# A transformer block's prologue: x's third tile on another queue, its statistics earlier, its copies split by features

## The chip, the cores and the metric

The kernel runs on one core of a Trainium2 chip. The metric is the device time of one execution in microseconds; smaller is better. The engines are named as in the profile: PE is TensorE (PEld its weight loads), DVE VectorE, ACT ScalarE, POOL GpSimd, SP SyncE. SyncE and ScalarE issue the transfers (DMAs), each on a queue of its own.

## The reference

x has 2048 rows of 576 bf16 elements. The block normalises x once and adds three terms:

```python
xn = _layernorm(x)                       # (x - mean) / sqrt(var + 1e-5), by rows
qkv = (xn @ wqkv)                        # 576 -> 3 * 576, 32 heads of 18
p = softmax(where(0 <= i - j < 256, q @ k.T * 18**-0.5, -1e9))
A = (p @ v) @ wo
B = (silu(xn @ w1) * (xn @ w3)) @ w2     # 576 -> 4608 -> 576
out = x + A + B
```

## The kernel before

**Tiling.** The 2048 rows are worked through in four chunks of 512, and a chunk in four tiles of 128 rows. For each chunk: V, q and k are projected (L491), then 36 units of the feed-forward's first half run (L759), with the attention's scores (L621), exponentials and products with V (L689) dealt between them, then the second half and the output (L832). The normalised rows are needed transposed, features on the partitions: `xnT`. From the second chunk on, this preparation happens under the work of the chunk before. For the first chunk nothing lies before it, and a prologue written out by hand does it. The change lies there.

**Order.** Every operation is put by `add` into one list; each engine runs its own operations in the order of that list, and waits on semaphores that are worked out from which buffers an operation reads and writes. So each engine is a queue in which one waiting instruction holds up all behind it.

**The prologue**, tiles 0 to 3 of x:

- `load_x` (L304) asks for a tile of 128 rows: tile 0 on SyncE's queue, tiles 1, 2, 3 on ScalarE's. SyncE's queue goes on with V's weights `wv` (L890, L894), then those of q and k (L920, L924; in the trace their target is `pt`), and later the feed-forward's (L328). GpSimd copies each tile's last 64 columns (L963), in tile order, as soon as it lands.
- `ln_stats` (L394, L397): VectorE takes the statistics of a tile in two halves of 288 columns and joins them. Tile 1's are taken by ScalarE instead (L385, L388). `ln_sqrt` (L367): ScalarE takes the root. `normalise`: VectorE takes its reciprocal (L372) and scales the tile (L411). The small buffers (`stats`, `mv`, `rstd`, `sd`) are two each, by turns.
- `xn_turn` (L426, L439): TensorE transposes a tile in ten small matmuls (five blocks of 128 features, each for two halves of 64 rows) into PSUM, and two copies bring it to `xnT`. A copy takes either some of the features of all 128 rows (blocks 0 and 1, or 2 to 4, each from a bank pair of its own), or, with `by_rows`, all features of 64 rows, both from one pair. Before the change tiles 0 and 1 are copied by features, both copies on ScalarE; tiles 2 and 3 by rows, one copy on ScalarE, one on VectorE.
- `proj_begin` and `proj_end`: V of a tile is 18 matmuls (L491), eight in a first part, ten in a second; the second part is put behind the transposes of the next tile. The first part takes feature blocks in order, two matmuls each, and waits for blocks 0 and 1 by one key (`xnTa`), for 2 and 3 by another (`xnTb`). V of a tile needs a bank pair until VectorE and ScalarE have moved it to `va` in four steps (L540, L542); those steps are kept in the lists `moves` and `late` and put where the code says.
- PSUM has eight banks, used in pairs: `JOBS[0]`, `JOBS[1]`, `JOBS[2]`, and `SC` (banks 6 and 7). `job()` hands the three pairs of `JOBS` out in turn.
- Ahead of all this, matmuls on constants (L902, L908, L914) fill TensorE's time. Behind V come q and k (L491 too, from `wp`), for which GpSimd deals the weights out (L946). `xn_swap` (L454) makes `xnS`, `xnT` with its partition halves exchanged, for the feed-forward.

The order around the change, before (the first `ln_stats` line of tile 2 and the `xn_turn` of tiles 2 and 3 are what moves or changes):

Of the kernel before, what the change touches and what calls it, by code (L numbers as in the profile page):

```python
# [5 lines left out]
dt = mybir.dt  # L6
# [38 lines left out]
class _Prog:  # L45
# [13 lines left out]
    def add(self, eng, fn, r=(), w=(), j=(), dma=None, after=()):  # L59
        deps = []  # L60
        for k in r:
            deps += self.bufs[k].writers
        for k in w:
            g = self.bufs.get(k)
            if g is not None:
                deps += g.ahead(eng)
        for k in j:
            g = self.bufs[k].before
            if g is not None:
                deps += g.ahead(eng)  # L70
        op = _Op(eng, fn, deps + list(after), dma)
        op.after = tuple(after)
        self.n[eng] += 1
        op.pos = self.n[eng]
        if dma is not None:
            self.dma_count[dma] = self.dma_count.get(dma, 0) + 16
            op.cnt = self.dma_count[dma]
        for k in r:
            self.bufs[k].readers.append(op)
        for k in w:  # L80
            self.bufs[k] = _Gen([op], self.bufs.get(k))
        for k in j:
            self.bufs[k].writers.append(op)
        for k in w:
            if self.bufs[k].before is not None:
                self.bufs[k].before.before = None
        self.ops.append(op)
        return op
# [76 lines left out]
def bass_parallel_sum__sliding_block__glu_gated_swiglu__prompt_kernel(  # L165
# [23 lines left out]
    HD = D // 2  # L189
# [6 lines left out]
    add = P.add  # L196

    with ExitStack() as es:

        def sb(name, shape, dtype=dt.bfloat16):  # L200
            return es.enter_context(nc.sbuf_tensor(name, shape, dtype))
# [4 lines left out]
        ident = sb("ident", [128, 128])  # L206
        xp = [sb(f"xp{i}", [128, 640 if i < TB else D]) for i in range(NXP)]
        xn = [sb(f"xn{i}", [128, 640]) for i in range(2)]
        stats = [sb(f"stats{i}", [128, 2, 6], dt.float32) for i in range(2)]
        mv = [sb(f"mv{i}", [128, 2], dt.float32) for i in range(2)]  # L210
        vpe = [sb(f"vpe{i}", [128, 1], dt.float32) for i in range(2)]
        rstd = [sb(f"rstd{i}", [128, 1], dt.float32) for i in range(2)]
# [66 lines left out]
        JOBS, SC = ((0, 1), (2, 3), (4, 5)), (6, 7)  # L279
# [3 lines left out]
        def job():  # L283
            ring.append(ring.pop(0))
            return ring[2]

        def half_bank(b):
            return PS[:, b, :].bitcast(dt.bfloat16)
# [11 lines left out]
        def load_x(t, eng="sp"):  # L300
            nonlocal xp_ctr
            s = xp_ctr % NXP
            xp_ctr += 1
            add(eng, lambda e: e.dma_start(xp[s][:, 0:D], x2[t * 128:(t + 1) * 128, :]), w=[("xp", s)], dma=f"xp{s}")  # L304
            return s
# [59 lines left out]
        def ln_sqrt(t, scale=1.0):  # L365
            i = t % 2
            add("act", lambda e: e.activation(sd[i][:], mv[i][:, 1:2], ACT.Sqrt, bias=eps[:], scale=scale),  # L367
                r=[("mv", i), "eps"], w=[("sd", i)])

        def ln_recip(t):  # L370
            i = t % 2
            add("dve", lambda e: e.reciprocal(rstd[i][:], sd[i][:]), r=[("sd", i)], w=[("rstd", i)])  # L372

        def ln_root(t):
            i = t % 2
            add("pool", lambda e: e.tensor_scalar(vpe[i][:], mv[i][:, 1:2], 1e-5, None, op0=ALU.add),
                r=[("mv", i)], w=[("vpe", i)])
            add("pool", lambda e: e.tensor_tensor(rstd[i][:], vpe[i][:], neghalf[:], ALU.pow),
                       r=[("vpe", i), "neghalf"], w=[("rstd", i)])
# [9 lines left out]
                r=[("xp", s), ("vpe", i)], w=[("mv", i), *keys])  # L389

        def ln_stats(t, s, part):
            i = t % 2
            if part < 2:
                add("dve", lambda e: e.bn_stats(stats[i][:, part, :], xp[s][:, part * HD:part * HD + HD]),  # L394
                    r=[("xp", s)], **{"j" if part else "w": [("stats", i)]})
                return
            op = add("dve", lambda e: e.bn_aggr(mv[i][:], stats[i][:]), r=[("stats", i)], w=[("mv", i)])  # L397
            if t >= TB:
                ln_root(t)
            return op  # L400
# [14 lines left out]
        def xn_turn(t, pairs, eng, between=(), by_rows=False):  # L415
            i = t % 2
            c, tt = divmod(t, TB)
            ranges = ((0, 2), (2, 5))
            for n, (k0, k1) in enumerate(ranges):
                for k in range(k0, k1):  # L420
                    for r in range(2):
                        r0 = 64 * r
                        b = pairs[n][r]
                        bv = half_bank(b)[:, 64 * k:64 * k + 64]
                        new = k == k0 and (n == 0 or pairs[0] != pairs[1])
                        add("pe", lambda e, bv=bv, r0=r0, k=k: e.transpose(  # L426
                            bv, xn[i][r0:r0 + 64, k * 128:(k + 1) * 128], ident[r0:r0 + 64, r0:r0 + 64],
                            tile_position=(r0, 0)),
                            r=[("xn" if k < 4 else "xnd", i), "ident"], **{"w" if new else "j": [("ps", b)]})
            for what in between:  # L430
                what()
            dst = xnT[:, c % 2, :, tt * 128:(tt + 1) * 128].rearrange("p k (r f) -> p k r f", f=64)
            for n, (k0, k1) in enumerate(ranges):
                b = pairs[n][0]
                src = PS[:, b:b + 2, :].bitcast(dt.bfloat16)[:, :, 0:320].rearrange("p r (k f) -> p k r f", f=64)
                d, s = dst[:, k0:k1, :, :], src[:, k0:k1, :, :]
                if by_rows:
                    d, s = dst[:, :, n, :], src[:, :, n, :]
                move = (lambda e, d=d, s=s: e.tensor_copy(d, s)) if eng[n] == "dve" else (lambda e, d=d, s=s: e.activation(d, s, ACT.Copy))  # L439
                add(eng[n], move, r=[("ps", b) for b in pairs[n]],  # L440
                    **({"j": [("xnT", c % 2, tt), ("xnTb", tt)] + [("xnTa", tt)] * by_rows} if n else
                       {"w": [("xnT", c % 2, tt), ("xnTa", tt), ("xnTb", tt)]}))
# [77 lines left out]
        def proj_end(later=None, late=None):  # L520
            if pend:
                c, what, banks, last = pend.pop()
                proj_part(c, what, banks, 1, last)
                proj_out(c, what, banks, later, late)
                return what

        def proj_begin(c, what, banks=None):
            banks = banks or job()
            last = proj_part(c, what, banks, 0)
            got = proj_end()  # L530
            pend.append((c, what, banks, last))
            return got
# [352 lines left out]

        xslot = {}
        for t in range(TB):
            xslot[t] = load_x(t, "act" if t else "sp")
        add("act", lambda e: e.preload_act_table_set("sqrt_and_others"))
        add("sp", lambda e: e.dma_start(  # L890
            wv[:, 0:4, :], A_wqkv[0:512, 2 * D:3 * D].rearrange("(kd p) f -> p kd f", p=128)),
            w=["wv"], dma="wv")
# [12 lines left out]
        def warm_halves(banks, cols):  # L905
            for r in range(2):
                rows = slice(64 * r, 64 * r + 64)
                add("pe", lambda e, b=banks[r], rows=rows, r=r: e.matmul(  # L908
                    PS[:, b, 0:cols], oq[rows, 0:128], oq[rows, 0:cols], start=True, stop=True, tile_position=(64 * r, 0)),
                    r=["oq0"], w=[("ps", banks[r])])  # L910
# [54 lines left out]
        moves, late = [], []  # L965
        for p in range(2):
            ln_stats(0, xslot[0], p)
# [4 lines left out]
        def normalise(t):  # L972
            ln_recip(t)
            ln_apply(t, xslot[t], (2,))

        normalise(0)
        xn_turn(0, (SC, JOBS[1]), ("act", "act"))
        for cols in (256, 256, 128):
            warm_halves(JOBS[0], cols)
        ln_stats(2, xslot[2], 0)  # L980
        ln_stats(2, xslot[2], 1)
        normalise(1)
        ln_stats(2, xslot[2], 2)
# [8 lines left out]
        proj_end(moves, late)  # L992
        proj_begin(0, ("v", 1))
        ln_sqrt(3)
        xn_turn(2, (SC, SC), ("act", "dve"), by_rows=True)
        normalise(3)
        moves.pop(0)()
        first = [late.pop(0)]
        proj_end(moves, late)
        proj_begin(0, ("v", 2))  # L1000
        xn_turn(3, (SC, SC), ("act", "dve"), first, by_rows=True)
        for move in moves + late:
            move()
        xn_swap(0, ("sp", "sp"))
        proj_end()
        proj_begin(0, ("v", 3), SC)
        deal_main(0, 0, 0, 2)
        deal_spread(0)
        deal_main(0, 1, 0, G)
# [47 lines left out]
        for c in range(NC):  # L1057
# [133 lines left out]
            for u in range(NF):  # L1191
# [11 lines left out]
                for n in range(9):  # L1203
# [9 lines left out]
                    op = unit_pairs(c, u, n, n + 1, b0[0])  # L1213
# [11 lines left out]
                if u in stat:  # L1225
                    t = (c + 1) * TB + stat[u]
# [4 lines left out]
                if u in apply:  # L1231
                    t = (c + 1) * TB + apply[u]
# [11 lines left out]
                if c == 0 and u == 18:  # L1244
                    rows = A_wo[0:4 * Dh, :].rearrange("(n d) f -> n d f", d=Dh)
                    add("sp", lambda e: e.dma_start(wo[126:128, 0:4, :], rows[:, 0:2, :].rearrange("n d f -> d n f")),
                        j=["wo"], dma="wo")
                    for p in range(2):
                        add("sp", lambda e, p=p: e.dma_start(wo[64 * p:64 * p + 64, 4, :], rows[:, 2:Dh, :]),
                            j=["wo"], dma="wo")  # L1250
# [13 lines left out]
            for item in p2_list(c):  # L1264
# [14 lines left out]
                elif n in (100, 120) and c + 2 < NC:  # L1279
                    t = (c + 2) * TB + (n == 120)  # L1280
# [34 lines left out]
```

## Time and profile before

| | us |
|---|---|
| three runs | 554.45, 554.74, 555.17 |
| their median | 554.74 |
| the profiled execution | 554.48 |
| its span in the trace | 552.7 |

| engine | busy us | share of the span |
|---|---|---|
| PE | 548.7 | 99% |
| PEld | 338.7 | 61% |
| DVE | 313.7 | 57% |
| ACT | 258.8 | 47% |
| POOL | 212.3 | 38% |

In the timeline's rows stand the start in microseconds from the span's start, the time from the first to the last of a group, the engine, the line, the operation, the tiles written and read, the shape and the count; in brackets, how long the engine was idle before it and what released it. The chain of waits lists, in order of time, the work that the end of the execution hung on. Rows of groups end in busy microseconds, mean nanoseconds of one instruction, and idle time before it. TensorE's clock was granted in full over the whole span.

### The profile page before, as it was taken

How to read it: one execution, taken by the hardware profiler on the slowest of the kernel's cores; microseconds unless marked ns; L12 is line 12 of the kernel's file. 1: busy time of each engine (PE TensorE's matmuls, PEld its weight loads, DVE VectorE, ACT ScalarE, POOL GpSimd, SP SyncE). 2: the span in 40 equal slices, each digit the busy share in tenths (PEclk: the TensorE clock that was granted, in tenths of full speed). 3: DMA queues.
4: the chain of work that ended last, by engine and by line, in shares of the span. 5: the costliest groups of instructions: out<-in, count | busy, mean ns of one | idle time of the engine just before them, and what ended most of it. 6: DMA issues, size and time to landing. Idle time of an engine off the chain costs nothing.

```text
span 552.7 us, 18355 instructions
## 1 busy us (share of the span) xinstructions
PE 548.7 (99%) x8071; PEld 338.7 (61%) x8071; DVE 313.7 (57%) x584; ACT 258.8 (47%) x360; POOL 212.3 (38%) x388
## 2 busy tenths in 40 slices
PE   8999999999999999999999999999999999999998
PEld 5555544777555544577765554559886555445776
DVE  8466797710468886651056988665105567866311
ACT  6456776000288567700047857760005784775000
POOL 6324675400047465530005656643001553663100
PEclk9999999999999999999999999999999999999999
DMA  9997899676577953758646875466763673541750
GB/s 253 209 199 167 197 221 202 138 200 182 141 144 145 177 135 102 176 143 208 182 111 140 172 146 146 112 155 167 194 179 87 138 173 102 152 110 52 195 152 23
DMA packets 128038, 86.00 MB, mean 156 GB/s; under 512 B 35702, under 2 KB 125646, under 8 KB 127958
## 3 DMA queue, kind: packets, MB, share of 16 engines
q1 hardware_dynamic: 89138, 62.80, 49.7%
q10 hardware_dynamic: 38820, 22.02, 15.7%
q8 instruction: 63, 1.03, 0.8%
q14 instruction: 17, 0.14, 0.1%
HBM read 71.29 MB, written 2.36 MB: 133 GB/s over the span
## 4 chain that ended last, share of the span: by engine, by line
PE 98%; DMA 1%; ACT 0%; DVE 0%; issue 0%
PE ps L759 51%; PE ps L832 29%; PE ps L491 10%; PE ps L621 6%; PE ps L689 3%; DMA xp<-in_A_x_dram 1%; DVE stats L394 0%; ACT hT L388 0%; ACT sd L367 0%; PE ps L426 0%; ACT xnT L439 0%; DVE ofin L854 0%; DVE mv L397 0%
## 5 line engine op out<-in xcount | busy, mean ns | idle before, releaser
L759 PE MATMUL ps<-xnT,w 64*128 64x512 bf16 x1400 | 185.3, 376 | 0.0
L759 PE MATMUL ps<-xnS,w 64*128 64x512 bf16 x1120 | 150.6, 376 | 0.0
L832 PE MATMUL ps<-w,hT 64*128 64x288 bf16 x2292 | 144.0, 282 | 0.0
L774 DVE SCALAR_TENSOR_TENSOR gs<-th,ps 128x512 bf16<-128x512 bf16 x144 | 97.9, 680 | 77.7 <-ACT th L768 77.2
L832 PEld LDWEIGHTS ps<-w,hT 64*128 64x128 bf16 x2292 | 117.1, 94 | 24.8 <-issue 0.2
L768 ACT ACTIVATE th<-ps 128x512 bf16<-128x512 f32 x144 | 85.7, 595 | 60.5 <-PE ps L759 59.3
L759 PEld LDWEIGHTS ps<-xnT,w 64*128 64x128 bf16 x1400 | 66.8, 94 | 63.7
L777 DVE SCALAR_TENSOR_TENSOR hT<-gs,ps 128x512 bf16<-128x512 bf16 x144 | 98.9, 687 | 5.0
L658 POOL TENSOR_TENSOR pt<-pt,mk 128x256 bf16<-128x256 bf16 (+1 forms) x143 | 85.6, 622 | 26.3 <-ACT pt L630 26.3
L630 ACT ACTIVATE pt<-ps 128x1024 bf16<-128x1024 f32 (+1 forms) x80 | 80.7, 1009 | 24.0 <-PE ps L621 23.3
L658 POOL TENSOR_TENSOR hT<-hT,mk 128x256 bf16<-128x256 bf16 (+1 forms) x52 | 30.3, 604 | 160.4 <-ACT hT L630 160.4
L759 PEld LDWEIGHTS ps<-xnS,w 64*128 64x128 bf16 x1120 | 53.6, 94 | 51.0
L504 ACT ACTIVATE stage<-ps 128x512 bf16<-128x512 f32 x16 | 9.6, 597 | 139.2 <-PE ps L491 139.2
L863 DVE TENSOR_TENSOR ofin<-ps,xp 128x288 bf16<-128x288 f32 x31 | 12.2, 451 | 98.2 <-PE ps L832 98.2
L621 PE MATMUL ps<-qv,kv 64*128 64x320 bf16 (+4 forms) x528 | 51.4, 260 | 0.0
L621 PEld LDWEIGHTS ps<-qv,kv 64*128 64x128 bf16 x528 | 26.2, 94 | 27.7 <-ACT pt L630 0.8
L491 PE MATMUL ps<-xnT,wp 64*128 64x512 bf16 (+1 forms) x360 | 38.4, 355 | 0.0
L722 DVE STREAM_TRANSPOSE od<-oq 128x256 bf16<-128x256 bf16 x64 | 25.4, 426 | 12.1 <-POOL oq L715 12.1
L630 ACT ACTIVATE hT<-ps 128x1024 bf16<-128x1024 f32 (+1 forms) x28 | 28.4, 1014 | 7.8 <-PE ps L621 7.6
L658 POOL TENSOR_TENSOR stage<-stage,mk 128x256 bf16<-128x256 bf16 (+1 forms) x44 | 24.9, 587 | 14.4 <-ACT stage L630 14.4
L630 ACT ACTIVATE stage<-ps 128x1024 bf16<-128x1024 f32 (+1 forms) x24 | 24.3, 1014 | 7.9 <-PE ps L621 7.8
L491 PEld LDWEIGHTS ps<-xnT,wp 64*128 64x128 bf16 x360 | 18.4, 94 | 14.3
(92 smaller groups left out, 394.2 us busy)
## 6 DMA issues: line engine op xcount, KB each, us to landing
w<-in_B_w_dram SPq DMA_DIRECT2D x210, 192.0 KB, 4.0
w<-in_B_w_dram ACTq DMA_DIRECT2D x70, 288.0 KB, 3.6
xp<-in_A_x_dram SPq DMA_DIRECT2D x29, 144.0 KB, 4.1
out_dram<-ofin SPq DMA_DIRECT2D x31, 72.0 KB, 2.0
xnS<-xnT SPq DMA_DIRECT2D x8, 256.0 KB, 5.0
oT<-od SPq DMA_DIRECT2D x56, 36.0 KB
pt<-in_A_wqkv_dram SPq DMA_DIRECT2D x4, 288.0 KB, 5.3
hT<-in_B_w_dram SPq DMA_DIRECT2D x6, 192.0 KB, 7.1
```

The lines of the kernel that those rows point to most:

```text
L491: op = add("pe", lambda e, out_=out_, st=st, mv=mv, n=n, r0=r0, first=first: e.matmul(out_, st, mv, start=first, stop=(part == 1 and n == ...
L621: add("pe", lambda e, r0=r0, out_=out_, kb=kb, q0=q0, nb=nb: e.matmul(out_, kb4[r0:r0 + 64, g, kb + NV - NB, :] if kb < 0 else kv[r0:r0 + ...
L630: add("act", lambda e: e.activation(pt_slot(sl)[:, :, 0:w], PS[:, SC[0]:SC[1] + 1, 0:w], ACT.Exp, scale=scale), r=[("ps", b) for b in SC], ...
L658: add("pool", lambda e, vb=vb, mm=mm: e.tensor_tensor(vb, vb, mm, ALU.mult), r=(key if n == 0 else []) + ["mk"], **{"w" if n == 0 else "j" ...
L689: add("pe", lambda e, p=p, q=q, pr=pr, sl=sl, g=g, pos=pos, q0=q0, nb=nb, col=col, first=first, n=n: e.matmul(PS[32 * q:32 * q + VW, banks ...
L722: add("dve", lambda e: e.transpose(od[i][:, g % 2, c0:c0 + CH // 2], oq[:, c0:c0 + CH // 2]), r=["oq", "oq0"], **{"j" if half or g % 2 els ...
L759: op = add("pe", lambda e, n=n, r0=r0, r=r, k=k, src=src: e.matmul(PS[:, b0 + r, :], wt[r0:r0 + 64, k, fl * 128:(fl + 1) * 128], src, star ...
L768: add("act", lambda e: e.activation(th[i][:], PS[:, bg, :], ACT.Tanh, scale=0.5), r=[("ps", bg)], w=[("th", i)])
L774: add("dve", lambda e: e.scalar_tensor_tensor(out=gs[i][:], in0=th[i][:], scalar=1.0, in1=PS[:, bg, :], op0=ALU.add, op1=ALU.mult), r=[("t ...
L777: add("dve", lambda e: e.scalar_tensor_tensor(out=hT[:, u, :], in0=gs[i][:], scalar=0.5, in1=PS[:, bu, :], op0=ALU.mult, op1=ALU.mult), r= ...
L832: op = add("pe", lambda e: e.matmul(PS[:, bank, 0:w], stat, move, start=new, stop=False, skip_group_check=True, **tile), r=keys, after=hel ...
L863: add("dve", lambda e: e.tensor_tensor(ofin[:, o, :], PS[:, bank, 0:HD], xp[xs[n]][:, d0:d0 + HD], ALU.add), r=[("ps", bank), ("xp", xs[n] ...
```

## The change

Four things are done in the prologue.

1. Tile 2 of x is asked for by SyncE, behind tile 0 and ahead of V's weights. ScalarE asks for tiles 1 and 3.
2. The first half of tile 2's statistics stands on VectorE ahead of tile 0's reciprocal, instead of behind tile 0's scaling. The statistics buffer has three copies for that.
3. Tile 2 is copied to `xnT` by features: blocks 0 and 1 by VectorE from `SC`, blocks 2 to 4 by ScalarE from `JOBS[1]`. Tile 3, still by rows, is transposed into `JOBS[1]`.
4. V of tile 2 is accumulated in `SC` and V of tile 3 in a pair of `JOBS` (it was the other way round), and two of the evacuations of V's tile 0 on ScalarE, not one, stand ahead of the copies of tile 3.

```diff
-        stats = [sb(f"stats{i}", [128, 2, 6], dt.float32) for i in range(2)]
+        stats = [sb(f"stats{i}", [128, 2, 6], dt.float32) for i in range(3)]
...
         def ln_stats(t, s, part):
-            i = t % 2
+            i, b = t % 2, t % 3
             if part < 2:
-                add("dve", lambda e: e.bn_stats(stats[i][:, part, :], xp[s][:, part * HD:part * HD + HD]),
-                    r=[("xp", s)], **{"j" if part else "w": [("stats", i)]})
+                add("dve", lambda e: e.bn_stats(stats[b][:, part, :], xp[s][:, part * HD:part * HD + HD]),
+                    r=[("xp", s)], **{"j" if part else "w": [("stats", b)]})
                 return
-            op = add("dve", lambda e: e.bn_aggr(mv[i][:], stats[i][:]), r=[("stats", i)], w=[("mv", i)])
+            op = add("dve", lambda e: e.bn_aggr(mv[i][:], stats[b][:]), r=[("stats", b)], w=[("mv", i)])
...
-            xslot[t] = load_x(t, "act" if t else "sp")
+            xslot[t] = load_x(t, "act" if t % 2 else "sp")
...
+        ln_stats(2, xslot[2], 0)
         normalise(0)
         xn_turn(0, (SC, JOBS[1]), ("act", "act"))
         for cols in (256, 256, 128):
             warm_halves(JOBS[0], cols)
-        ln_stats(2, xslot[2], 0)
         ln_stats(2, xslot[2], 1)
         normalise(1)
...
         ln_sqrt(3)
-        xn_turn(2, (SC, SC), ("act", "dve"), by_rows=True)
+        xn_turn(2, (SC, JOBS[1]), ("dve", "act"))
         normalise(3)
         moves.pop(0)()
-        first = [late.pop(0)]
+        first = [late.pop(0) for _ in range(2)]
         proj_end(moves, late)
-        proj_begin(0, ("v", 2))
-        xn_turn(3, (SC, SC), ("act", "dve"), first, by_rows=True)
+        proj_begin(0, ("v", 2), SC)
+        xn_turn(3, (JOBS[1], JOBS[1]), ("act", "dve"), first, by_rows=True)
         for move in moves + late:
             move()
         xn_swap(0, ("sp", "sp"))
         proj_end()
-        proj_begin(0, ("v", 3), SC)
+        proj_begin(0, ("v", 3))
```

## The prediction

> **What bounds the kernel now.** I read the page's head and chain first, then the chain of waits inside the first 22 us, because the diff touches nothing later.
>
> ```profile
> span 552.7 us, 18355 instructions
> PE 98%; DMA 1%; ACT 0%; DVE 0%; issue 0%
> ...
> 0.79 2.78 DMA xp<-in_A_x_dram
> 3.59 0.83 DVE stats L394 x2
> 4.45 0.22 DVE mv L397
> ...
> 5.78 0.30 ACT sd L367
> ...
> 6.52 0.71 PE ps L491 x8
> ...
> 10.20 10.59 PE ps L491 x118
> ```
>
> The first two lines are the page's: TensorE carries 98% of the chain. The rest (start, us, what) is the prologue. One tile of x has to land (3.57) and pass through statistics, root, normalising, transposing and a copy before V's first matmul at 6.52; from then on the chain lies on TensorE. So only two things can move the end: the start at 6.52, or holes in TensorE's queue behind it. The holes show where the same work takes unequal time:
>
> ```profile
> 7.30 1.28 PE L491 MATMUL ps<-wv,xnT 64*128 64x288 bf16 x18
> 8.41 0.31 PE L426 MATMUL ps<-ident,xn 64*128 64x64 bf16 x10
> 8.64 1.41 PE L491 MATMUL ps<-wv,xnT 64*128 64x288 bf16 x18
> 10.12 1.28 PE L491 MATMUL ps<-wv,xnT 64*128 64x288 bf16 x18
> 9.38 0.36 PEld L491 LDWEIGHTS ps<-wv,xnT 64*128 64x128 bf16 x8 [0.26 <-ACT xnT L439]
> ```
>
> These are TensorE's rows in the timeline. Each 18 matmuls are the second half of one V tile and the first half of the next. The middle group takes 1.41 instead of 1.28: 0.13 us lost, and the weight load at 9.38, the first of V's tile 2, names ScalarE's copy of the transposed tile as what it waited for. That is the one hole of this stretch that the diff can reach.
>
> **The change, part by part.** *Copies by features.* Tile 2's transposes went to one bank pair and each engine copied one half of the rows, so V's tile 2 needed both copies. Now VectorE copies features 0 to 255 from one pair, ScalarE the other 384 from another, and V's first two of four matmul pairs need only VectorE's.
>
> ```profile
> 8.76 0.33 DVE L439 COPY xnT<-ps 128x320 bf16<-128x320 bf16 x1
> 8.71 0.30 ACT L367 ACTIVATE sd<-mv,eps 128x1 f32<-128x1 f32 x1 [0.61 <-DVE mv L397]
> 8.91 0.42 ACT L439 ACTIVATE xnT<-ps 128x320 bf16<-128x320 bf16 x1
> 10.24 0.44 ACT L439 ACTIVATE xnT<-ps 128x320 bf16<-128x320 bf16 x1 [0.62 <-PE ps L426]
> L439 ACT ACTIVATE xnT<-ps 128x384 bf16<-128x384 bf16 x2 | 1.0, 485 | 0.0
> ```
>
> TensorE would be at V's tile 2 by 9.38 - 0.13 = 9.25. VectorE's copy of 256 has no row: its bounds are nothing and the 0.33 of the copy of 320, and the nearest row is the latter; it ends by 8.76 + 0.33 = 9.09, and 9.25 is met. ScalarE's copy grows to 485 ns: begun at 8.91 it ends at 9.40, and its reader is the third pair, at 9.25 + 2 x 0.123 = 9.50 (nine pairs run from 7.30 to 8.41, 0.123 each). So the 0.13 goes whole even if nothing else moved; what is late next is TensorE itself. Tile 3's transposes now go where ScalarE's copy (to 9.40) was, which ends before they come: 10.12 less the 0.23 that transposes take (8.41 to 8.64) less 0.13 is 9.76.
>
> *Two evacuations ahead of ScalarE's copy of tile 3*, where one stood.
>
> ```profile
> 10.70 2.08 ACT L540 ACTIVATE va<-ps 64x288 bf16<-64x288 f32 x5
> 6.00 0.77 ACT L439 ACTIVATE xnT<-ps 128x256 bf16<-128x256 bf16 x2
> ```
>
> One holds ScalarE for 2.08/5 = 0.42. The idle 0.62 before the copy at 10.24 must cover it, and that copy will be wanted at 10.11. From its start a 384 copy holds ScalarE 0.39 (the pair at 6.00, 256 then 384, takes 0.77; the 256 takes the other half). Begun at 8.91 the queue is 8.91 + 0.39 + 2 x 0.42 = 10.14: 0.03 late, and V's tile 3 waits for exactly this. If the root of tile 3 comes 0.15 earlier (next part) there is 0.12 of room. Bounds 0 to +0.03; I take 0.
>
> *Half of tile 2's statistics ahead of the first root's reciprocal*, with a third statistics buffer.
>
> ```profile
> 5.02 0.16 DVE L372 RECIPROCAL rstd<-sd 128x1 f32<-128x1 f32 x1 [0.36 <-ACT sd L367]
> 5.58 0.81 DVE L394 BATCH_NORM_STATS2 stats<-xp 128x6 f32<-128x288 bf16 x2
> 6.31 0.14 DVE L372 RECIPROCAL rstd<-sd 128x1 f32<-128x1 f32 x1
> 6.86 0.20 DVE L397 BATCH_NORM_AGGREGATE mv<-stats 128x2 f32<-128x12 f32 x1
> 6.97 0.41 DVE L394 BATCH_NORM_STATS2 stats<-xp 128x6 f32<-128x288 bf16 x1
> ```
>
> This adds a wait: if the tile has not landed, VectorE stands, with the reciprocal, tile 0's normalising, its transposes and V's start queued behind it. Landed in time, the instruction starts 0.11 after the aggregate (6.86 to 6.97), at 4.56, and lets the next start after 0.73/2 = 0.365 (5.58 to 6.31 for two), at 4.93. The reciprocal waits for its root until 5.02 anyway: cost nothing, under cover of that 0.36 idle. Without the cover it costs 0.37. The latest harmless landing is 5.02 - 0.37 = 4.65.
>
> Behind it, the second reciprocal moves from 6.31 to its own root, 5.78 + 0.30 = 6.08, say 6.11. That gains 0.20 on VectorE for tile 1 and, through the aggregates, for tile 2 and the root of tile 3. TensorE gains nothing by it: tile 1's transposes stand in its queue behind the eight matmuls that began at 6.52.
>
> *x's third tile on SyncE's queue, second.*
>
> ```profile
> 1.25 0.42 SPq L890 DMA_DIRECT2D wv<-in_A_wqkv_dram  x1
> 5.24 0.21 POOL L963 COPY xp<-xp 128x32 f32<-128x32 f32 x1 [1.11 <-DMA xp<-in_A_x_dram]
> wv<-in_A_wqkv_dram SPq DMA_DIRECT2D x1, 576.0 KB, 4.7
> q1 hardware_dynamic: 131, 0.14, 60.7%
> q1 hardware_dynamic: 153, 0.16, 74.8%
> q10 hardware_dynamic: 70, 0.07, 25.5%
> 5.34 1.14 SPq L920 DMA_DIRECT2D pt<-in_A_wqkv_dram  x2
> 8.13 4.85 SPq L328 DMA_DIRECT2D w<-in_B_w_dram  x6
> ```
>
> GpSimd's copy at 5.24 waits for tile 2, so today it lands just before. The q rows are packets: SyncE's queue (q1) from 1.8 to 3.0, then SyncE's and ScalarE's (q10) from 3.0 to 3.74. A tile is 128 packets. SyncE's first 128 went out by 3.0 and landed at 3.57; its second 128, now V's weights, by 3.74. Put tile 2 there and it lands near 3.74 + 0.57 = 4.3, 0.35 before 4.65. The far bound is today's 5.24.
>
> The Trainium skill, "DMA: Bandwidth & Descriptors", section "Queues, rings and completion order", says that each DMA engine takes turns between the queue rows that have work. By that, second on SyncE's row is served like second on ScalarE's. The 153 against 70 packets, while ScalarE's queue owed two tiles, disagree here; I go by the rows. By the rule the sum would be that of the late tile below.
>
> V's weights wait for 128 packets more on their queue while ScalarE's carries as many fewer. They land at 1.25 + 4.7 = 5.95 today, and V starts at 6.52. The bounds are no delay and the whole 0.74 of the second 128 packets, which is 6.69, 0.17 too late; since all queues together carry the same bytes ahead of them, I take the lower end and no cost. SyncE's other issues slip by one slot, 0.46 (0.79 to 1.25): they end at 6.48 + 0.46 = 6.94, before the weights at 8.13. ScalarE loses an issue, and its queue then waits for tile 1 as before. GpSimd's small copies wait for the tiles in order and get tiles 2 and 3 sooner. V's tiles 2 and 3 swap bank pairs: two jobs, the first two of q, still lie between tile 3 and the next user of its pair. These cost nothing.
>
> **Sum.** -0.13 + 0 + 0 + 0 = -0.13 us. Does it last? What the first big matmuls need is timed by transfers:
>
> ```profile
> L454 SPq DMA_DIRECT2D xnS<-xnT x2: 537/566/596, 13.1 to 13.7; - x2
> DMA to landing us min/median/max: 6.2/6.5/6.9
> 21.47 0.39 PE L759 MATMUL ps<-xnS,w 64*128 64x512 bf16 x2
> ```
>
> The swapped copies of xnT, second issue at 13.7, land by 20.6 and are read at 21.47: 0.9 of room against 0.13. So it lasts. The profiled execution took 554.48 (1.8 around its span of 552.7), which becomes 554.35. The three runs' median is 554.74, 0.26 above it; I predict on it: 554.74 - 0.13 = 554.6.
>
> **The rivals.** *Tile 2 is late (slower).* If position in the queue doesn't help and it lands at 5.24, the reciprocal moves to 5.24 + 0.37 = 5.61, 0.59 later, and V's start with it; the 0.13 still goes. Net +0.46: 555.2. It decides from a landing at 4.65 on. For: the diff puts the wait on the longest path. Against: the packet rows. To pass +0.2% (1.1 us, about what a measurement of this kernel can tell from no change) the landing would have to be at 4.65 + 1.1 + 0.13 = 5.9.
>
> *The hole is refilled.* ScalarE's extra evacuation, or V's weights by up to 0.17, takes the gain: 554.61 + 0.03 to 554.61 + 0.17, so 554.6 to 554.8. For: 0.03 over in the queue above if the root comes no earlier. Against: VectorE's 0.20.
>
> *VectorE's 0.20 reaches TensorE too.* Then 0.33 goes: 554.4. For: tiles 1 to 3 are all normalised earlier. Against: the transposes stand behind matmuls in TensorE's queue.
>
> *It doesn't do what it says.* V's start on tile 2 still waits for both copies: 554.74. Against: tiles 0 and 1 are already copied by features.
>
> **How the numbers follow.** Forecast 0.70, late tile 0.10, refilled 0.10, the larger gain 0.04, both copies still awaited 0.03, something unseen 0.03. None of the named cases leaves +-0.2%; for what is unseen, and for the spread of runs (0.29 under and 0.43 over the median), I give faster by more 0.05, within 0.2% 0.91, slower by more 0.04. The range goes from the larger gain less the lower spread, 554.4 - 0.29 = 554.1, to the late tile, 555.2, with 0.1 for a VectorE instruction at its full length: 555.3.
>
> **What would show it.** Right: the three groups of 18 all at 1.28, no weight load of V waiting for a copy near 9.3, the reciprocal still near 5.02 with half of tile 2's statistics before it, GpSimd's third small copy near 4.4, and the chain's block of L491 ending at 20.66 instead of 20.79 (10.20 + 10.59). The late tile would show as VectorE waiting for a transfer before that statistics row, and V starting near 7.1. Wrong altogether would be a difference that arises after 22 us, where nothing was changed.

## The result: slower by a microsecond, outside the range

| | median us | runs |
|---|---|---|
| before, measured beside it | 554.57 (554.35 to 555.17) | 22 |
| after | 555.55 (554.25 to 556.97) | 22 |
| profiled execution, before and after | 554.48 and 555.57 | |

The ratio is 1.0018, 95% interval 1.0012 to 1.0025. That is within 0.2% or just past it; 554.6 had been forecast, in a range up to 555.3.

The profile after: first the page's head and its share line, then, from the chain of waits inside the first 22 us, the pieces that matter (start, us, what).

```profile
span 553.8 us, 18354 instructions
...
PE 98%; DMA 1%; SPq 0%; DVE 0%; issue 0%
```

```profile
1.72 5.86 DMA wv<-in_A_wqkv_dram
7.57 0.04 issue
7.62 0.66 PE ps L491 x8
...
11.11 10.74 PE ps L491 x114
```

Before, the chain ran through a tile of x, statistics, root and scaling to V's start at 6.52. All that has left the chain. In its place stands one transfer: V's weights, asked for at 1.72 and landed at 7.57. TensorE's rows of the timeline, and VectorE's and GpSimd's, say what became of the rest:

```profile
7.62 0.66 PE L491 MATMUL ps<-wv,xnT 64*128 64x288 bf16 x8 [1.22 <-DMA wv<-in_A_wqkv_dram]
8.35 1.28 PE L491 MATMUL ps<-wv,xnT 64*128 64x288 bf16 x18
9.69 1.28 PE L491 MATMUL ps<-wv,xnT 64*128 64x288 bf16 x18
11.03 1.28 PE L491 MATMUL ps<-wv,xnT 64*128 64x288 bf16 x18
```

```profile
4.66 0.41 DVE L394 BATCH_NORM_STATS2 stats<-xp 128x6 f32<-128x288 bf16 x1
5.10 0.16 DVE L372 RECIPROCAL rstd<-sd 128x1 f32<-128x1 f32 x1
...
6.19 0.17 DVE L372 RECIPROCAL rstd<-sd 128x1 f32<-128x1 f32 x1
4.34 0.50 POOL L963 COPY xp<-xp 128x32 f32<-128x32 f32 x2 [0.20 <-DMA xp<-in_A_x_dram]
...
9.73 0.29 DVE L439 COPY xnT<-ps 128x256 bf16<-128x256 bf16 x1 [1.16 <-PE ps L426]
```

V starts 1.10 later (7.62 against 6.52). Its third group of 18 starts 0.91 later (11.03 against 10.12), since the 0.13 at tile 2 is gone and the first eight took 0.05 less. The block of L491 ends at 11.11 + 10.74 = 21.85 instead of 20.79, 1.06 later; the times of the two profiled executions differ by 1.09. So all of the loss arises before 22 us, and it begins with the weights.

The trace marks 16 parts of a transfer as they complete. The parts of V's weights:

| kernel | asked | completed |
|---|---|---|
| before | 1.25 | all 16 between 5.42 and 5.97 |
| after | 1.72 | 11 by 5.95, then 6.17, 6.24, 6.40, 7.17, 7.57 |

Most parts are as early as ever. A few lag, and V waits for the last one.

The packet records of the two traces say a little more. Of the packets of 1152 bytes (one row of x or of V's weights) that began between 3.9 and 6.0 us, the median took 0.05 us in both kernels. The longest took 0.16 before and 0.83 after, where it began at 4.67. (Between 3.0 and 3.9 us it is the other way round, but milder: 0.32 before, 0.13 after.) From 6.6 us on the last of V's packets begin one at a time, 0.04 to 0.05 apart, up to 6.91. This looks like one of the 16 shares standing behind a slow packet; the records do not say which packet belongs to which share, so it is not shown.

### The profile page after: what moved, and what is told of

It reads as the page before. It is cut to its first block, busy times and chain, and to the rows that moved or that the text cites. A ratio compares the mean times of both kernels' runs of the same rounds, so it can differ in the third digit from the quotient of the medians.

```text
span 553.8 us, 18354 instructions
## 1 busy us (share of the span) xinstructions
PE 548.8 (99%) x8071; PEld 330.8 (60%) x8071; DVE 313.7 (57%) x584; ACT 258.9 (47%) x360; POOL 212.7 (38%) x388
## 4 chain that ended last, share of the span: by engine, by line
PE 98%; DMA 1%; SPq 0%; DVE 0%; issue 0%
PE ps L759 51%; PE ps L832 29%; PE ps L491 10%; PE ps L621 6%; PE ps L689 3%; DMA wv<-in_A_wqkv_dram 1%; SPq L304 0%; PE ps L426 0%; DVE ofin L854 0%
## 5 line engine op out<-in xcount | busy, mean ns | idle before, releaser
L759 PE MATMUL ps<-xnT,w 64*128 64x512 bf16 x1400 | 187.7, 376 | 0.0
L759 PE MATMUL ps<-xnS,w 64*128 64x512 bf16 x1120 | 152.8, 376 | 0.0
L832 PEld LDWEIGHTS ps<-w,hT 64*128 64x128 bf16 x2292 | 112.4, 94 | 29.4 <-issue 0.2
L621 PE MATMUL ps<-qv,kv 64*128 64x320 bf16 (+4 forms) x528 | 53.1, 260 | 0.0
L491 PE MATMUL ps<-xnT,wp 64*128 64x512 bf16 (+1 forms) x360 | 38.6, 355 | 0.0
L491 PEld LDWEIGHTS ps<-xnT,wp 64*128 64x128 bf16 x360 | 17.6, 94 | 15.3 <-POOL wp L946 0.4
```

Of the source, the lines that this page charges most:

```text
L491: op = add("pe", lambda e, out_=out_, st=st, mv=mv, n=n, r0=r0, first=first: e.matmul(out_, st, mv, start=first, stop=(part == 1 and n == ...
L621: add("pe", lambda e, r0=r0, out_=out_, kb=kb, q0=q0, nb=nb: e.matmul(out_, kb4[r0:r0 + 64, g, kb + NV - NB, :] if kb < 0 else kv[r0:r0 + ...
L759: op = add("pe", lambda e, n=n, r0=r0, r=r, k=k, src=src: e.matmul(PS[:, b0 + r, :], wt[r0:r0 + 64, k, fl * 128:(fl + 1) * 128], src, star ...
L832: op = add("pe", lambda e: e.matmul(PS[:, bank, 0:w], stat, move, start=new, stop=False, skip_group_check=True, **tile), r=keys, after=hel ...
```

## The experiments

The medians of before, measured beside these kernels: 554.54 (experiments 1 to 4), 554.52 (5 to 8), 554.63 (9 to 12), 554.56 (13 to 15).

### 1. Only the queue changes; 2. all but the queue and the order of statistics; 3. all but the queue

Experiment 1 is the kernel before with this edit:

```diff
-            xslot[t] = load_x(t, "act" if t else "sp")
+            xslot[t] = load_x(t, "act" if t % 2 else "sp")
```

> The kernel before with one line changed: SyncE asks for tile 2 of x, second. Theory (the weights are late): V's weights land 1 to 2 us later than before, a few of their sixteen parts far behind the rest, and V starts at 7.4 to 7.8; with V so late the hole of 0.13 closes by itself, so the time is that of the changed kernel, 555.3 to 555.8, with runs more than 1.5 us apart. Rival (another part of the change costs the time: the banks, the evacuations, the statistics): V starts at 6.5 and the time is 554.5 to 554.7.

Measured: 556.27 (555.28 to 558.12, 8 runs), ratio 1.003 (1.0014 to 1.0047). Four of the runs had a granted clock of 0.997 (557.08 to 558.12; on this below), the other four are 555.28 to 555.45. From its chain and timeline:

```profile
1.71 5.63 DMA wv<-in_A_wqkv_dram
...
7.39 0.66 PE L491 MATMUL ps<-wv,xnT 64*128 64x288 bf16 x8 [0.87 <-DMA wv<-in_A_wqkv_dram]
...
9.46 1.28 PE L491 MATMUL ps<-wv,xnT 64*128 64x288 bf16 x18
```

The queue's edit alone brings the loss: V starts 0.87 later than before, and the four runs at the full clock are 0.74 to 0.91 above the median of before. It also warns against a quick reading: here the copies are still by rows, and the hole at tile 2 is closed all the same (1.28), because a late V gives every copy time. So the 1.28 of the kernel after does not show that the new copies brought anything. For that the next one is needed.

Experiment 2 is the kernel after with these two lines put back as they were:

```diff
-            xslot[t] = load_x(t, "act" if t % 2 else "sp")
+            xslot[t] = load_x(t, "act" if t else "sp")
...
-        ln_stats(2, xslot[2], 0)
         normalise(0)
...
+        ln_stats(2, xslot[2], 0)
         ln_stats(2, xslot[2], 1)
```

> The changed kernel with the queue and the order of the statistics as before, so copies by features, banks and the two evacuations alone. Theory (the weights are late): V starts at 6.52 as before, the three groups of 18 matmuls take 1.28 each, time 554.4 to 554.5 with a spread like that of before. Rival (another part costs): 555 or more, with the loss behind V's start.

Measured: 554.35 (554.19 to 554.75, 11 runs), ratio 0.9997 (0.9989 to 1.0006). TensorE's rows of its timeline with one weight load, then the piece of its chain that ends the block of L491:

```profile
6.46 0.71 PE L491 MATMUL ps<-wv,xnT 64*128 64x288 bf16 x8 [0.21 <-ACT xnT L439]
7.23 1.27 PE L491 MATMUL ps<-wv,xnT 64*128 64x288 bf16 x18
8.57 1.27 PE L491 MATMUL ps<-wv,xnT 64*128 64x288 bf16 x18
9.92 1.34 PE L491 MATMUL ps<-wv,xnT 64*128 64x288 bf16 x18
...
10.56 0.39 PEld L491 LDWEIGHTS ps<-wv,xnT 64*128 64x128 bf16 x8 [0.17 <-ACT xnT L439]
```

```profile
10.00 10.63 PE ps L491 x118
```

V starts on time, the hole is closed (1.27), and the block ends at 20.63 instead of 20.79: 0.16 earlier. The sum behind it: the start is 0.06 earlier, tile 2 gives 0.14 (1.27 for 1.41), and 0.06 is lost again at tile 3 (1.34 for 1.28), whose first weight load now waits for ScalarE's copy. The medians differ by 0.19 in its favour. The interval of the ratio doesn't exclude no change. It is the lowest median of all the kernels run.

Experiment 3 is the kernel after with the first line only put back, so that VectorE waits early for a third tile that is second on ScalarE's queue.

> The changed kernel with tile 2 asked for by ScalarE again, so its statistics now wait for the tile. By the prediction's rival of the late tile: VectorE waits for the transfer until about 5.2, the reciprocal starts near 5.6, V at 7.1, the hole is gone, time 554.57 + 0.46 = 555.0, weights in by 6.0. Rival (another part costs): as the changed kernel or slower, 555.5 to 556.

Measured: 555.14 (554.69 to 557.22, 11 runs), ratio 1.0014 (1.0005 to 1.0024). Its profiled execution, at 556.14, is one of its slower ones. The chain, and the issue of V's weights (KB, us to landing):

```profile
1.24 5.24 DMA xp<-in_A_x_dram
...
6.88 0.15 DVE rstd L372
...
8.37 0.71 PE ps L491 x8
```

```profile
wv<-in_A_wqkv_dram SPq DMA_DIRECT2D x1, 576.0 KB, 6.2
```

The late-tile rival's mechanism is real: with the tile late, the early statistics hold up the reciprocal and V. The kernel differs from experiment 2 by the order of the statistics alone, and its median is 0.79 higher; it is 0.60 above before, where 0.46 had been worked out. The profile can't confirm that price: the tile landed at 6.48 instead of near 5.2, and V started 1.85 later. In the kernel after it doesn't happen, since there the tile lands in time. Two details matter for what follows. In this execution 15 parts of the tile came by 5.50 and the last at 6.48; and V's weights, though asked for at 1.25, landed only at 7.50, by one late part too (15 had come by 5.74).

### 4 to 8. What makes the weights lag: the queue, the company, the tile ahead?

Experiment 4 splits V's weights in the kernel after: half on SyncE's queue behind the third tile, half on ScalarE's behind the second and the fourth. The theory was that the lag comes from one queue carrying 576 KB alone.

```diff
+        for n, eng in enumerate(("sp", "act")):
+            add(eng, lambda e, n=n: e.dma_start(wv[:, 2 * n:2 * n + 2, :], A_wqkv[256 * n:256 * n + 256, ...]), ...)
```

> The changed kernel with V's weights (feature blocks 0 to 3) asked for in two halves, one on SyncE's queue behind tile 2, one on ScalarE's behind tile 3. Theory (the weights are late because their queue carries them alone): they land by 6.1, V starts at 6.6, time 554.4 to 554.5, narrow. Rival (the late parts of the transfer come from the memory and not from the queue): still some parts near 7.5, time 555.2 to 555.6.

```profile
wv<-in_A_wqkv_dram SPq DMA_DIRECT2D x1, 288.0 KB, 5.4
wv<-in_A_wqkv_dram ACTq DMA_DIRECT2D x1, 288.0 KB, 5.7
```

Measured: 555.77 (555.2 to 557.61, 11 runs), ratio 1.0023 (1.0014 to 1.0031). Both halves land past 7.1, V starts at 7.57. Half the bytes on either queue lag as much: that theory falls.

Experiment 5 is the kernel before with x's fourth tile asked for by SyncE behind V's weights instead of by ScalarE. ScalarE's queue then empties early, as it does in the kernel after, while the weights keep their place.

```diff
-        for t in range(TB):
+        for t in range(TB - 1):
...
+        xslot[3] = load_x(3, "sp")
```

> The kernel before with tile 3 of x asked for by SyncE behind V's weights, so that V's weights keep their place (second on SyncE's queue) and ScalarE's queue runs empty some 1.2 us earlier. Theory A (V's weights lag when no x tile shares the transfer engines with them): some of their sixteen parts lag, V starts after 7, time 555.2 to 556. Theory B (they lag because of their own later place or issue): they land by 5.95 or sooner, V starts at 6.5, time 554.5 to 554.8 (tile 3 lands near 6.9, still in time).

```profile
1.26 0.42 SPq L890 DMA_DIRECT2D wv<-in_A_wqkv_dram  x1
...
wv<-in_A_wqkv_dram SPq DMA_DIRECT2D x1, 576.0 KB, 4.7
...
6.52 0.71 PE L491 MATMUL ps<-wv,xnT 64*128 64x288 bf16 x8 [0.21 <-ACT xnT L439]
```

Measured: 554.88 over eleven runs (ten are 554.38 to 555.29, one took 970.18 at a granted clock of 0.558), ratio 1.0004 (0.9995 to 1.0013). The weights land at 5.94, so the earlier end of ScalarE's queue isn't what makes them lag. It doesn't settle whether they lag when they travel alone, because x's third tile, landed at 5.84, still travelled beside them here. Experiments 6 and 9 below settle that: x's fourth tile travelled beside the weights there (landed at 6.66 and 7.54), and they lagged all the same.

Experiments 6 and 7 are the kernel before with one useless transfer more on SyncE's queue ahead of the weights, of 16 rows of x or of 128, into a buffer that isn't read before it is filled again.

```diff
+        add("sp", lambda e: e.dma_start(xp[6][0:16, 0:D], x2[0:16, :]), w=[("xp", 6)], dma="extra")
```

> The kernel before with one small extra transfer (16 rows of x into a buffer that nothing reads) on SyncE ahead of V's weights: their issue slips by 0.46 us, their place by one packet on each transfer engine, ScalarE's queue is as before. If the later issue is what hurts: parts lag, V starts after 7, 555.2 to 556. Theories of place (B, 128 packets) and of sharing (A): weights in by 6.1, V at 6.5, 554.5 to 554.7.

> The kernel before with a whole extra tile of x (128 packets into a buffer that nothing reads) on SyncE ahead of V's weights, and ScalarE's three tiles as before. Theory B (place): parts lag as in the changed kernel, V starts at 7.3 to 7.8, 555.3 to 556. Theory A (sharing): ScalarE's tiles still run beside the weights, no part lags by more than 0.6, the whole lands 0.3 to 0.5 later by the extra bytes, V at 6.5 to 6.7, 554.5 to 554.8.

The chain of 6, and the issue of the weights in 7:

```profile
1.71 6.04 DMA wv<-in_A_wqkv_dram
...
7.79 0.66 PE ps L491 x8
```

```profile
wv<-in_A_wqkv_dram SPq DMA_DIRECT2D x1, 576.0 KB, 7.1
```

Measured: 556.26 (556.01 to 557.11, 5 runs), ratio 1.0033 (1.002 to 1.0045), and 557.35 (557.17 to 558.26, 5 runs), ratio 1.0053 (1.004 to 1.0065). One eighth of the packets does at least as much harm as the move did; a whole tile extra costs 1 us more, so bytes ahead can add to the loss, but it doesn't need them. What 6 has in common with the kernel after is not the bytes ahead but the moment: asked for at 1.71, a slot of 0.46 later.

Experiment 8 is the kernel after with 28 more matmuls on constants ahead of V, to see whether TensorE's standing costs anything besides the time it stands.

```diff
-        for cols in (256, 256, 128):
+        for cols in (256, 256, 128) + (256,) * 14:
```

> The changed kernel with 28 more covering matmuls of 256 columns behind the first transposes, 1.5 us of work, so that TensorE is busy until about 7.6 whether the weights are there or not. Theory (the runs above 556.5, whose granted clock was 0.997, are those in which TensorE stood so long that its clock was taken back): no run with a lower clock, none above 556.3, median 555.5 to 555.7. Rival (those runs are only those with the latest weights): runs above 556.5 as often as in the changed kernel, 4 of 22.

Measured: 563.28 (562.75 to 563.72, 5 runs), ratio 1.0154. It couldn't answer: V starts at 7.64 as in the kernel after, the clock is full, and its median is 7.7 us above that kernel's. TensorE's waits (us in total, times, longest) show where most of it went, and name no releaser:

```profile
PE ps L759 <- issue: 5.5, 6, 1.1
```

### 9 to 12. Only the moment

Experiment 9 is the kernel before with one thing different: SyncE's request for V's weights waits until GpSimd has set a small constant. No transfer is added or moved to another place.

```diff
-        add("pool", lambda e: e.memset(eps[:], 1e-5), w=["eps"])
+        held = add("pool", lambda e: e.memset(eps[:], 1e-5), w=["eps"])
...
-            w=["wv"], dma="wv")
+            w=["wv"], dma="wv", after=(held,))
```

> The kernel before with V's weights held back on SyncE until GpSimd's small memset of 1e-5 is done (about 1.6), so that they are asked for at about 1.7 instead of 1.25; no transfer is added or moved. Theory (the moment of asking is what hurts): parts of the weights lag, V starts after 7, time 555.2 to 556.2. Rival (what hurts is a further transfer ahead of the weights on their queue): no part lags by more than 0.6, V at 6.5 to 6.6, 554.5 to 554.7.

```profile
1.63 6.42 DMA wv<-in_A_wqkv_dram
...
8.10 0.75 PE ps L491 x8
```

Measured: 557.42 (556.04 to 558.85, 6 runs), ratio 1.0052 (1.0041 to 1.0063). Asked for 0.38 later, the weights land 2.1 later. Five of its six runs have a granted clock of 0.997 (on this below), so its time is not the price of the delay alone. Experiment 11 holds them until a later memset of GpSimd's, moved up for it:

> As the run with the later request, but held until GpSimd's first memset of va is done, so that V's weights are asked for at about 2.1. Theory of the moment: they lag at least as much as when asked for at 1.7, V at 7.5 to 8.5, 555.5 to 557. Rival (a further transfer ahead): V's weights land some 0.4 to 0.8 later as a whole, no single part lags by more than 0.6, V at 6.5 to 6.9, 554.5 to 555.

```profile
2.00 6.23 DMA wv<-in_A_wqkv_dram
```

Measured: 557.53 (556.02 to 557.6, 5 runs), ratio 1.0045 (1.0033 to 1.0057). Once past the moment, another 0.37 adds only 0.18 to the landing. Experiment 10 is the kernel after with the q and k weights' transfers held until the first reciprocal, so that nothing large is prepared right behind V's weights:

> The changed kernel with the transfers that SyncE asks for behind V's weights (those for q and k) held back until VectorE's first reciprocal, about 5.1 instead of 3.45. Theory (making ready the later, many-pieced transfers takes from the weights in flight): no part of V's weights lags, all in by 6.1, V at 6.6. Rival (the lag arises in the weights' own transfer): parts lag to 7 or more, V at 7 to 7.8, as in the changed kernel. The time says little here, because q and k then wait for their weights: 555 to 557 either way.

Measured: 556.02 (555.5 to 557.11, 11 runs), ratio 1.0027 (1.0019 to 1.0036). V's weights still land at 7.25 in the profiled execution (its slowest), V starts at 7.29: the transfers for q and k behind them are not the cause. Experiment 12, meanwhile, is experiment 2 with one evacuation ahead of ScalarE's copy of tile 3 instead of two:

> The kernel with the copies and the banks alone, and one evacuation ahead of ScalarE's copy of tile 3 as before instead of two. By the prediction's sum the second evacuation costs 0 to 0.03: the time is that of the copies with two, 554.35, within 0.1, three groups of 18 at 1.28, V at 6.5. Rival (the second evacuation pays for itself because V's first banks come free sooner): slower than the copies with two by 0.1 or more, with a wait of the first q matmul.

Measured: 554.44 (554.21 to 554.74, 11 runs), ratio 0.9998 (0.9989 to 1.0006), beside 554.35 with two: the second evacuation costs nothing that can be seen. Its three groups of 18 take 1.34, 1.28 and 1.40, where 1.28 each had been expected: the hole at tile 2 is closed here too, and another stands at tile 3.

### 13 to 15. The moment, or the order of the two engines' requests?

Experiment 13 is the kernel after, but ScalarE asks for V's weights, second on its queue, and SyncE keeps the third tile second on its own:

```diff
         for t in range(TB):
             xslot[t] = load_x(t, "act" if t % 2 else "sp")
+            if t == 1:
+                add("act", lambda e: e.dma_start(wv[:, 0:4, :], ...), w=["wv"], dma="wv")
-        add("sp", lambda e: e.dma_start(wv[:, 0:4, :], ...), w=["wv"], dma="wv")
```

> The kernel after, but ScalarE asks for V's weights as its second request (behind the second tile, ahead of the fourth), at about 1.24 us; SyncE asks for the first and the third tile. Theory of the moment (what counts is that V's weights are asked for no later than any other engine's second request, about 1.25): they land by 6.1 without lagging parts and V starts at 6.5 to 6.7; with the 0.13 of the hole gone the median is 554.3 to 554.7, or up to 555.2 if the third tile lands past 4.65. Rival (the place behind the third tile, or SyncE's queue as such, matters): the weights land past 7, V starts past 7.1, 555.2 to 556.5.

```profile
1.24 0.46 ACTq L890 DMA_DIRECT2D wv<-in_A_wqkv_dram  x1
...
6.58 0.71 PE L491 MATMUL ps<-wv,xnT 64*128 64x288 bf16 x8
7.36 1.28 PE L491 MATMUL ps<-wv,xnT 64*128 64x288 bf16 x18
8.70 1.28 PE L491 MATMUL ps<-wv,xnT 64*128 64x288 bf16 x18
10.04 1.41 PE L491 MATMUL ps<-wv,xnT 64*128 64x288 bf16 x18
...
9.86 0.20 PEld L426 LDWEIGHTS ps<-ident,xn 64*128 64x128 bf16 x10 [0.20 <-DVE xn L411]
...
10.75 0.39 PEld L491 LDWEIGHTS ps<-wv,xnT 64*128 64x128 bf16 x8 [0.24 <-ACT xnT L439]
```

Measured: 554.39 (554.18 to 554.49, 11 runs), ratio 0.9994 (0.9986 to 1.0003). Here the weights stand on the other queue, the third tile is where the change wants it, and the loss is gone: besides the queue, which experiment 4 had cleared, the weights got back the moment of their request. But tile 3 pays 0.13 at the end. Its transposes wait for VectorE's scaling, and its first weight load for ScalarE's copy. The three groups take 3.97 together, exactly what they take before the change.

Experiments 14 and 15 are the kernel before with holds like that of 9: in 14 on both SyncE's request for the weights and ScalarE's for the third tile, in 15 on the third tile alone.

> The kernel before, with ScalarE's request for the third tile and SyncE's request for V's weights both held until GpSimd has set its small constant, about 1.63 us. Theory of order (V's weights lag only when they are asked for after ScalarE's second request): no lag, they land at 5.95 + 0.4 = 6.3 or so and V starts at 6.5 to 6.7, or later only by the third tile's own delay; 554.5 to 555. Theory of the clock on the wall (any request from 1.6 us on lags, whatever its neighbours do): the weights land past 7.2, V starts past 7.2, 555.3 to 558.

> The kernel before, with only ScalarE's request for the third tile held until about 1.63 us; V's weights are asked for at 1.25 as before. By either theory V's weights land by 6.0 and V starts at 6.5 to 6.6. By the theory of the clock on the wall the third tile now has the lagging parts and lands past 5.6; its turn comes at about 8.4, so that the median is 554.5 to 554.9. If V's weights lag here too (past 6.6), both theories fall and the two queues' requests only do well when they are made together.

The chain of 14; the issue of the weights and the chain of 15:

```profile
1.63 6.72 DMA wv<-in_A_wqkv_dram
...
8.40 1.10 PE ps L491 x8
```

```profile
wv<-in_A_wqkv_dram SPq DMA_DIRECT2D x1, 576.0 KB, 4.7
1.63 4.34 DMA xp<-in_A_x_dram
```

Measured: 14: 556.76 (555.65 to 557.87, 6 runs), ratio 1.0034 (1.0021 to 1.0046); the profiled execution is the slowest. 15: 554.83 (554.44 to 555.31, 11 runs), ratio 1.0004 (0.9995 to 1.0013). With both held, the order and the distance between the two requests are as before, and the weights lag. With the tile alone held, the weights are on time (1.26 + 4.7). The tile itself, asked for at 1.63, lands at 5.97, 0.79 later than before, but as a whole: its 16 parts come between 5.26 and 5.97. So the order between the queues isn't what counts.

All profiled executions together:

| V's weights asked for | kernels | landed | V's start |
|---|---|---|---|
| 1.24 to 1.26 | before, 2, 5, 12, 13, 15 | 5.6 to 6.3 | 6.45 to 6.58 |
| 1.25 | 3 | 7.5 | (8.37, by the tile) |
| 1.63 to 2.00 | after, 1, 4, 6, 7, 8, 9, 10, 11, 14 | 7.2 to 8.8 | 7.3 to 8.8 |

## Why the prediction was wrong

**The step that failed** is the one on V's weights: "The bounds are no delay and the whole 0.74 of the second 128 packets, which is 6.69, 0.17 too late; since all queues together carry the same bytes ahead of them, I take the lower end and no cost." They landed at 7.57, 0.88 past that upper bound. Most parts of the transfer did what the sum of bytes said: 11 of 16 landed by 5.95, as if nothing had been moved. But a transfer is done when its last part is, and the bound was made from what went ahead in the queue (128 packets), not from how far the last part of a late transfer strays. Experiment 6 shows that the packets ahead were the wrong measure: with 16 rows ahead the weights landed at 7.75, with the 128 of the kernel after at 7.57. The next sentence of the prediction, that SyncE's other issues "slip by one slot, 0.46", held for those (the last by 0.50). V's weights slip by the same slot (1.25 to 1.72), and experiment 9 shows that such a slip suffices for the loss; I had priced them by the queue's bytes and not by the slot.

**The rival nearest to it**, the refilled hole, named the right transfer but priced it with the same bound, 0.17, where V started 1.10 later. The late tile, to which the range reached, is borne out by experiment 3, in a kernel where the tile is late; here it landed at 4.28, against 4.3 forecast and 4.65 allowed.

**Point by point.**
- *Copies by features*, -0.13: right at tile 2, shown by experiment 2 (-0.14). But "the 0.13 goes whole" failed: where V starts on time, a hole opens at tile 3. The three groups of 18 take 3.97 together before, 3.88 in experiment 2, 4.02 in 12 and 3.97 in 13, so these profiles show at most 0.09 to gain. The kernel after shows neither, since the late V would have closed the holes anyway (experiment 1). VectorE's copy of 256 takes 0.29, inside its bounds.
- *The second evacuation*, 0 to +0.03: nothing seen (12 against 2). It isn't what opens the hole at tile 3, which is larger with one evacuation (0.12) than with two (0.06).
- *Half statistics under VectorE's idle time*: right. They begin at 4.66, and the reciprocal follows at 5.10; of its 0.08 over 5.02 all is the first tile's landing, as the first statistics begin at 3.67 instead of 3.59. The second reciprocal came earlier as forecast (6.19 against 6.31; 6.11 had been said).
- *The rule of turns.* The third tile landed at 4.28, against 5.18 when it was second on ScalarE's queue. The place isn't the only reason: in experiments 6, 9 and 11 it was still second on ScalarE's and landed at 3.83 to 3.97, with V's weights asked for later. In 13, second on SyncE's with the weights as early as before, it landed at 4.13. The Trainium skill, "DMA: Bandwidth & Descriptors", section "Queues, rings and completion order", says that each DMA engine takes turns between the queue rows that have work. The kernel after agrees: from 2.5 to 4.0 us both queues moved as much, and its fourth tile, second on ScalarE's queue, landed at 4.57. So the 153 against 70 packets that the prediction set against the rule are not general, and what made the queues unequal before is not shown. The packets of the kernel after in that stretch:

```profile
q10 hardware_dynamic: 258, 0.26, 51.1%
q1 hardware_dynamic: 263, 0.27, 51.0%
```

- *"What is late next"* was answered for the hole but not for the start: the first matmul had 6.52 - 5.95 = 0.57 of room on its weights, and I spent that room on a price that no row of the trace had shown.
- *Behind V*, 0.15 more is lost up to 21.85 (1.06 against 0.91). The one wait that the timeline names there is a weight load for q and k:

```profile
16.06 5.51 PEld L491 LDWEIGHTS ps<-xnT,wp 64*128 64x128 bf16 x60 [0.40 <-POOL wp L946]
```

  GpSimd deals those weights out as they land. That this is the 0.15 was not tested.

**What stays open** is why V's weights lag when they are asked for from 1.63 us on. Shown is that the lag doesn't need one queue or the other (4), more bytes ahead (9), or a journey alone (6, 9), and that neither q's and k's transfers behind (10) nor the order of the engines' requests (14) makes it. Experiment 9 moves the weights' request by 0.38 us and, with it, only what SyncE asks for behind them, so asking later is enough to bring the lag. It is not a rule for every request: before the change x's fourth tile is asked for at 1.72, and its parts all land between 5.82 and 6.47; the tile of experiment 15 doesn't stray either. Nor is it sharp: in experiment 3 the weights had one lagging part although asked for at 1.25, one run of before beside the experiments took 556.82 at the full clock, and the kernel after had single runs as low as 554.25. The traces do show slow packets wherever the moment is late: of the packets of 1152 bytes begun between 3.9 and 6.0 us, the longest took 0.41 to 1.24 us in these ten profiles, 0.11 to 0.29 in the six on time and 0.31 in experiment 3, beside a median of 0.05 in all. What slows them was not found. A sum over bytes and queues can't give it.

## What to carry to other kernels

Where a transfer is the first operand of the bottleneck, its request keeps its moment: price a slot lost ahead of it by how far its last part can stray, and move the less urgent request behind it or to the other engine (experiment 13 has everything the change wanted, without its loss, though with no gain over before that can be told apart). When several edits come together, run each alone: here the lowest median belongs to the copies and their evacuations alone (554.35), and the group times of the whole change would have credited the copies with a hole that the delay itself had closed.

## What had not been expected of the hardware

**Parts that lag.** 0.38 us of delay in asking became 2.1 us of delay in landing (9), while 12 of the 16 parts had come by 6.35, the 5.97 of before and the delay.

**The clock.** Runs above 556.5 of the kernel after (4 of 22), and half of experiment 1's, have a mean granted clock of 0.997 instead of 1. The profile of experiment 9 fell on such a run. Its windows (TensorE's busy us and granted clock among the columns), and below them those of before and after over the same stretch:

```profile
core 0: us, PE busy (x) PEld busy (x) DVE busy (x) ACT busy (x) POOL busy (x), PEclk, DMA share, GB/s
5.10:8.50 3.40, 1.42 (x29) 0.78 (x28) 2.69 (x10) 1.83 (x6) 0.21 (x1) 1.00 1.06 314
...
8.60:11.90 3.30, 3.30 (x48) 2.32 (x44) 0.86 (x4) 1.26 (x4) 0.93 (x3) 0.50 1.13 241
```

```profile
5.10:8.50 3.40, 2.63 (x61) 1.77 (x60) 3.22 (x12) 2.64 (x8) 0.42 (x2) 1.00 1.12 327
```

```profile
5.10:8.50 3.40, 1.62 (x40) 1.08 (x40) 3.15 (x11) 2.12 (x7) 0.00 (x0) 1.00 1.09 318
```

In experiment 9 the clock is at one half from about 8.55 to 11.95, 3.4 us, just as V begins, after 3.4 us in which TensorE was busy for 1.42. Half speed for 3.4 us is 1.7 us of work lost. With 1.62 busy the profiled execution of the kernel after escaped it; the kernel before, with 2.63, never showed it: in all its 92 runs beside the experiments the clock is 1. The Trainium skill, "TensorE: Matmul & The Clock Gate", "Part 1: The HAM clock gate", describes a window of about 3.4 us that runs free of the kernel, with half speed after an idle one. The length agrees with these rows, and so does that only some runs are hit. But TensorE was not idle for a window here: it worked for 1.42 of 3.4 us, so an idle window is more than these rows needed. A late V thus costs twice: its delay, and in some runs another 1.7. In experiment 1 the four runs at 0.997 are 1.6 to 2.8 above the other four.

**Waits without a releaser.** Adding 28 matmuls ahead of V (8) cost 7.7 us, mostly in six stalls of up to 1.1 us on TensorE, spread between 100 and 500 us. Their cause was not looked for.
